# A block-recurrent attention and ELU-MLP kernel on one core: each engine's order from a table instead of a list scheduler

## Chip, cores and metric

The kernel runs on one core of one Trainium2 chip. The metric is the device time of one execution in microseconds (us), lower is better. The profile is one execution recorded by the hardware profiler. PE is TensorE's matmuls, PEld its weight loads, DVE is VectorE, ACT ScalarE, POOL GpSimd, SP SyncE; SP and, for three transfers, ACT issue the DMAs.

## What is computed

Eight batches of eight heads; 512 rows of x and 32 rows of state per head, 64 wide. Attention goes both ways, and the result feeds an MLP with an ELU between its two products.

```python
B, H, S, Ns, D = (8, 8, 512, 32, 64)
scores = scale * np.matmul(x, state.transpose(0, 1, 3, 2))      # softmax over the last axis -> a
xread = np.matmul(a, state)
scores2 = scale * np.matmul(state, x.transpose(0, 1, 3, 2))     # softmax over the last axis -> a2
sread = np.matmul(a2, x)
...
x = concatenate([xread, sread], axis=2), as (B * 544, 512)
h = x @ w_in                                                    # 512 -> 2048
g = np.where(h > 0.0, h, alpha * (np.exp(np.minimum(h, 0.0)) - 1.0))
return (g @ w_out).astype(np.float32)                           # 2048 -> 512
```

The two weights arrive as float64 and are turned into float32 words on the chip.

## The kernel before

The kernel folds the state rows into w_in: for a batch it first makes m = state x w_in (`make_m`, `make_three`, in four chunks of 512 columns of w_in), so that `ffn1` is softmax weights times m. `ffn1` and the second product `ffn2` use Strassen-like schemes: sums of blocks on DVE and POOL replace an eighth of the matmuls, and the second product does so twice (`Second`, steps named "second"). The parts are:

- `start()` (L1189): batches 0 and 1 plainly, while sixteen blocks of the weights arrive by DMA (1 MB each) and are converted by ACT and DVE (`convert`, L1129); converted w_in is written back to DRAM in eight halves for later fetches.
- `ffn2_1` (L1455), then `batch(b)` for b = 2 to 7 (L1522): `ffn1_chunk` four times, then `ffn2` (L1358), which also prepares batch b+1 at the boundary: scores, both softmaxes, x loaded anew, the transposed weights moved within SBUF by 16 small DMAs (`move_state`, L829), the state's read-out (`state_read`, L842), and its first chunks of m from fetched halves of w_in (`fetch`, L671).
- `states()` (L1634): the 256 state rows of all batches through the MLP.

None of these functions emits an instruction. Each records *steps* in `Plan` (L87), numbered in the order of recording: 2862 of them, 753 for PE, 1019 for DVE, 626 for ACT, 126 for POOL, 338 for SP. A step has an engine, an assumed cost, the steps that it depends on (from overlapping regions of its buffers), the PSUM banks that it opens or closes, and for a DMA its bytes and rate (`DMA_COST`, L23). A PE step is a group of matmuls, and each matmul call is two records in the profile (a "second" step is four calls, eight records).

`Plan.order` (L368) then makes up to three passes. `set_due` (L218) gives every step a due time, backwards from PE's steps laid end to end in the order of recording and from the steps that followed one another in a bank in the pass before. `run` (L241) plays the plan forward as a list scheduler: at each moment the engine that can start first takes a step that is ready, PE the one recorded earliest, POOL strictly in the order of recording, the others the one due earliest. PSUM banks are given out as the play goes on, the one that came free first to the next step that opens one. The pass that ends first in its own reckoning is kept, and its steps are emitted sorted by their planned start (L1712). The emission order is the order of every engine's queue; an engine runs its queue strictly in order. Where the play sees PE idle in its first 40 us, it puts filler matmuls (`fill`, L1703).

```python
for _, n, op in able[e]:
    if e == POOL and op is not in_turn[0]:
        continue
    ...
    if start <= at + 1e-9:
        return at, op
```

Steps that the prediction names, by number:

- Start. PE: 25 and 79 scores of batches 0 and 1; 58 state turned (batch 1); 73, 76 x turned (batch 1); 185, 187, 199, 201 turned softmax rows; 189, 203 read-outs; 65, 69, 118, 122 and 96, 100, 126, 130 the first eight tiles of ffn1 of batches 0 and 1; 111, 114, 141, 144, 155, 158, 229, 232 make_m, one half of w_in each. DVE: 26 to 41 softmax of batch 0 (37 its reciprocal, 38 and 40 multiply, 39 and 41 transpose); 107 part of a conversion; 59 copy of a turned state. ACT: 60 the other copy; 36 a sum ahead of the reciprocal; 66, 70, 71 ELU; 84, 88 exponentials of batch 1's softmax; 134 a conversion; 195, 196 exponentials of batch 1's row softmax, which 199 and 201 read.
- Batch 4. PE: 1374 make_three, 1383 state_read, 1445 the next make_three; SP: 1310 to 1325 move_state, 1402 to 1404 fetch; POOL: 1330 to 1333, 1379 to 1382, 1450 to 1457 sums of m.
- Batch 7's boundary. PE: 2353 to 2378 "second" steps; DVE: 2356 to 2375.

Of the kernel before, what the change touches and what calls it, by code (L numbers as in the profile page):

```python
# [20 lines left out]
PE, DVE, ACT, POOL, SP = "PE", "DVE", "ACT", "POOL", "SP"  # L21
# [13 lines left out]
def elements(ap):  # L35
    n = 1
    for k in ap.shape[1:]:
        n *= k
    return n


class Bank:
# [44 lines left out]
class Plan:  # L87
# [13 lines left out]
    def __init__(self, psum):  # L101
        self.psum, self.ops, self.banks, self.fixed = psum, [], [], []
        self.rows, self.writers, self.readers, self.masks = {}, {}, {}, {}
        self.places = {}

    def track(self, ap):
        self.rows[ap.tensor.name] = ap.ap[0][0]
# [88 lines left out]
    def prepare(self):  # L196
        for op in self.ops:
            op.users = []
            op.turn = self.places.get(op.number, op.number)
        for op in self.ops:  # L200
            for d in op.deps:
                d.users.append(op)
        self.opening = {}
        self.closing = {}
        for b in self.banks:
            self.opening.setdefault(b.first, []).append(b)
            self.closing.setdefault(b.last, []).append(b)
        self.kept = {}
        for b in self.fixed:
            self.kept.setdefault(b.first, []).append(b.fixed)  # L210
        self.all_banks = min([op.number for op in self.kept], default=0)
# [3 lines left out]
            return 0.1  # L215
        return self.LAG[a.engine].get(b.engine, 0.0)

    def set_due(self, after):  # L218
        at = 0.0
        for op in self.ops:  # L220
            op.due = 1e6 + op.number
        for op in sorted((op for op in self.ops if op.engine == PE), key=lambda op: op.turn):
            op.due = at
            at += op.cost
        follow = {}
        for a, b in after:
            follow.setdefault(a, []).append(b)
        for op in reversed(self.ops):
            took = op.cost
            if op.moved:  # L230
                took = op.cost + self.LANDING + op.moved / op.rate
            for u in op.users:
                op.due = min(op.due, u.due - self.lag(op, u) - took)
            for u in follow.get(op, ()):
                op.due = min(op.due, u.due - self.lag(op, u) - took)
            op.due -= op.nudge
        for op in self.ops:
            if op.rank is not None:
                op.due = op.rank - 1e6

    def run(self, until=0.0):  # L241

        waiting = {op: len(op.deps) for op in self.ops}
        ready = dict.fromkeys(self.ops, 0.0)
        free_at = dict.fromkeys(ENGINES, 0.0)
        for e in (PE, ACT, SP):
            free_at[e] = 0.7
        able = {e: [] for e in ENGINES}
        coming = {e: [] for e in ENGINES}
        banks = [(0.0, i) for i in range(self.BANKS)]  # L250
        fixed = {b.fixed for b in self.fixed}
        openers = sorted((op for op in self.ops if op in self.opening), key=lambda op: op.turn)
        oldest, opened = 0, set()
        in_turn = [op for op in self.ops if op.engine == POOL]
        holder, after, done, fills, lanes = {}, [], [], [], []
        port, holds, wire, shape, spare = 0.0, None, 0.0, None, None

        def release(op):
            heapq.heappush(coming[op.engine], (ready[op], op.number, op))

        def bank_time(op):

            if op in self.kept:
                free = [t for t, i in banks if i in self.kept[op]]
                return max(free) if len(free) == len(self.kept[op]) else None
            need = len(self.opening[op])
            if op is not openers[oldest] and op.number > self.all_banks:
                need += self.KEPT_BANKS
            free = choice(op)
            return free[need - 1][0] if need <= len(free) else None  # L270

        def choice(op):
            if op.number < self.all_banks:
                return banks
            return [b for b in banks if b[1] not in fixed]

        def pick(e):

            at = free_at[e]
            if not able[e] and coming[e]:  # L280
                at = max(at, coming[e][0][0])
            while able[e] or coming[e]:
                while coming[e] and coming[e][0][0] <= at + 1e-9:
                    _, n, op = heapq.heappop(coming[e])
                    bisect.insort(able[e], ((op.turn if e == PE else op.due), n, op))
                later = [coming[e][0][0]] if coming[e] else []
                for _, n, op in able[e]:
                    if e == POOL and op is not in_turn[0]:
                        continue
                    start = max(at, ready[op])  # L290
                    if op.port:
                        start = max(start, port + 0.01 * (e == POOL == holds))
                    if op in self.opening or op in self.kept:
                        t = bank_time(op)
                        if t is None:
                            continue
                        start = max(start, t)
                    if op.moved and len(lanes) >= 8:
                        start = max(start, lanes[-8] + 0.1)
                    if start <= at + 1e-9:  # L300
                        return at, op
                    later.append(start)
                if not later:
                    return None
                at = min(later)
            return None

        for op in self.ops:
            if not waiting[op]:
                release(op)  # L310
        while len(done) < len(self.ops):
            best = None
            for e in ENGINES:
                found = pick(e)
                if found and (best is None or found[0] < best[0] - 1e-9):
                    best = found + (e,)
            assert best is not None, "no operation is ready"
            at, op, e = best
            if e == POOL:
                in_turn.pop(0)  # L320
            able[e].remove(((op.turn if e == PE else op.due), op.number, op))
            if e == PE:
                t = free_at[PE]
                while at < until and t + 0.5 < at:
# [4 lines left out]
                        fills.append((t, spare.index, 1))  # L329
                    t += 0.3  # L330
            for bank in self.opening.get(op, ()):
                t, i = got = choice(op)[0]
                banks.remove(got)
                bank.index = i
                if i in holder:
                    after.append((holder[i], op))
                opened.add(op)
            if op in self.kept:
                banks = [b for b in banks if b[1] not in self.kept[op]]
                after += [(holder[i], op) for i in self.kept[op] if i in holder]  # L340
            while oldest < len(openers) and openers[oldest] in opened:
                oldest += 1
            if e == PE and (op.spare or op.name == "make_m"):
                spare = op.spare
            if e == PE and op.shape != shape:
# [11 lines left out]
            for u in op.users:  # L357
                ready[u] = max(ready[u], op.end + self.lag(op, u))
                waiting[u] -= 1
                if not waiting[u]:  # L360
                    release(u)
            for b in self.closing.get(op, ()):
                bisect.insort(banks, (op.end + self.LAG[op.engine].get(PE, 0.0), b.index))
                holder[b.index] = op
        self.after, self.fills = after, fills
        return done

    def order(self, passes, until=0.0):  # L368
        self.prepare()
        after = []  # L370
        best = None
        for _ in range(passes):
            self.set_due(after)
            try:
                done = self.run(until)
            except AssertionError:
                assert best is not None
                break
            last = max(op.end for op in done)
            after = self.after  # L380
            if best is None or last < best[0]:
                steps = [(op.start, op.number, op, op.end) for op in done]
                best = (last, sorted(steps), list(self.fills), [b.index for b in self.banks])
        self.last, steps, fills, index = best
        for b, i in zip(self.banks, index):
            b.index = i
        for at, n, op, end in steps:
            op.start, op.end = at, end
        return [s[2] for s in steps], fills

@with_exitstack
def kernel(
# [728 lines left out]
    def store(b, h, o):  # L1121
        rows = out_b[b, 0:S].rearrange("(p r) c -> p r c", r=R)
        dma(rows[:, 2 * h : 2 * h + 2], o.o_sb[h], kind="store")
        plan.ops[-1].nudge = 0

    def words(raw):
        return [raw.rearrange("p n (j w) -> p n j w", w=2)[:, :, :, i] for i in range(2)]

# [580 lines left out]
            )  # L1709
        )  # L1710

    steps, fills = plan.order(3, 40.0)  # L1712
    for op in steps:
        while fills and fills[0][0] <= op.start:
            fill(*fills.pop(0)[1:])
# [32 lines left out]
```

## Time and profile before

| what | value |
|---|---|
| median of 3 runs | 697.64 us (696.82 to 1012.53) |
| span of the profiled execution | 695.1 us, 14567 instructions |
| granted TensorE clock | 1.000 |
| PE, PEld, DVE, ACT, POOL busy | 684.7, 590.5, 572.4, 302.2, 112.7 us |
| first and last matmul | 1.36 us, last one ends at 690.4 us |
| DMA | 78.55 MB, 113 GB/s on the mean |

The profiled execution's own time is its span of 695.1 us and what lies around it, 2.5 us if it took as long as the median. In a line of the timeline, the columns are: start, length of the merged piece, engine, line, operation, what is written and read, how many records; in brackets the engine's idle time before it and what ended it. Nearly all instructions have line L466, since one helper emits them, so they are told apart by the buffers' names: ps is PSUM, sec, s, g, xr, aT, m, o, t_w, w_out, w_half and xe are parts of the on-chip buffer. L1706 is the filler. In a table by stage each engine has its busy time and, in brackets, its number of records; the last three columns are the granted clock, the DMA share and GB/s. A group's line ends with its busy time, the mean length of one in ns, and the idle time ahead of it.

### The profile page before, as it was taken

The page shows a single profiled execution, that of the slowest core. Times are in us where ns is not written, and L with a number is a line of the kernel's source. Part 1 is how long each engine was busy: PE and PEld are TensorE (multiplying, and loading weights), DVE is VectorE, ACT ScalarE, POOL GpSimd, SP SyncE. Part 2 cuts the span into 40 slices and gives each one's busy share as a digit, 9 for nine tenths or more (in the row PEclk, how much of TensorE's full clock was granted, in tenths as well). Part 3 has the DMA queues.
Part 4 walks back from the last instruction along what each step waited for, and adds up shares of the span by engine and source line. Part 5 has one row for each costly group of instructions (what it writes and reads, how often), then busy time and mean ns, then how long its engine had stood idle before and what let it go on. Part 6 is the DMA issues. An engine that isn't in the chain of part 4 may idle for free.

```text
span 695.1 us, 14567 instructions
## 1 busy us (share of the span) xinstructions
PE 684.7 (98%) x5782; PEld 590.5 (85%) x5782; DVE 572.4 (82%) x1019; ACT 302.2 (43%) x640; POOL 112.7 (16%) x133
## 2 busy tenths in 40 slices
PE   8999999999999999999999999999999999999997
PEld 7544468889988998889988998899888998899996
DVE  4999899979949994999679995999499966997640
ACT  4999883003057213732275215731373217600530
POOL 0200000002430151104230143015110423000000
PEclk9999999999999999999999999999999999999999
DMA  8858774202281507440572218250745043200300
GB/s 222 271 190 260 255 219 99 61 31 91 72 223 41 122 19 235 83 122 4 167 166 74 50 39 244 53 123 18 240 77 123 1 154 122 61 1 32 122 8 24
DMA packets 111268, 78.55 MB, mean 113 GB/s; under 512 B 89184, under 2 KB 92768, under 8 KB 111200
## 3 DMA queue, kind: packets, MB, share of 16 engines
q1 hardware_dynamic: 108988, 77.06, 39.6%
q8 instruction: 46, 0.75, 0.5%
q10 hardware_dynamic: 2212, 0.56, 0.4%
q14 instruction: 22, 0.18, 0.1%
HBM read 61.34 MB, written 13.11 MB: 107 GB/s over the span
## 4 chain that ended last, share of the span: by engine, by line
PE 90%; ACT 4%; DMA 4%; DVE 1%; issue 1%; ACTq 0%
PE ps L466 90%; ACT sec L466 2%; DMA xe<-in_x_dram 1%; DMA t_w<-in_moe_w_out_dram 1%; DMA g<-in_x_dram 1%; ACT t_w L466 1%; DVE w_half L466 0%; ACT o L466 0%; DVE t_w L466 0%; DVE sec L466 0%; ACT w_half L466 0%; ACTq L466 0%; ACT g L466 0%; ACT m L466 0%; ACT s L466 0%
## 5 line engine op out<-in xcount | busy, mean ns | idle before, releaser
L466 PE MATMUL ps<-aT,m 128*128 128x256 f32 (+1 forms) x568 | 147.9, 405 | 0.2
L466 PE MATMUL ps<-w_out,g 128*128 128x128 f32 (+1 forms) x864 | 144.2, 314 | 0.0
L466 PEld LDWEIGHTS ps<-w_out,g 128*128 128x128 f32 x864 | 126.3, 191 | 12.4 <-issue 4.2
L466 PEld LDWEIGHTS ps<-aT,m 128*128 128x128 f32 x568 | 106.2, 190 | 29.6 <-issue 14.1
L466 DVE TENSOR_TENSOR o<-o,ps 128x128 f32<-128x128 f32 (+2 forms) x239 | 67.3, 286 | 41.2 <-PE ps L466 40.5
L466 ACT COPY o<-ps 128x128 f32<-128x128 f32 (+2 forms) x70 | 23.1, 335 | 145.6 <-PE ps L466 139.6
L466 POOL TENSOR_TENSOR xr<-xr,small 128x512 f32<-128x512 f32 x24 | 30.0, 1271 | 335.1 <-DVE small L466 171.3
L466 PE MATMUL ps<-sec 128*128 128x128 f32 x560 | 74.8, 277 | 0.0
L466 PEld LDWEIGHTS ps<-sec 128*128 128x128 f32 x560 | 68.5, 192 | 4.0 <-DVE o L466 3.7
L466 POOL TENSOR_TENSOR m<-m 128x256 f32<-128x256 f32 x72 | 60.5, 861 | 27.1 <-ACT m L466 25.7
L466 PE MATMUL ps<-t_w,s 128*128 128x128 f32 (+1 forms) x432 | 64.5, 298 | 0.0
L466 ACT ACTIVATE xe<-ps 128x512 f32<-128x512 f32 x96 | 54.9, 602 | 19.4 <-PE ps L466 12.8
L466 PEld LDWEIGHTS ps<-t_w,s 128*128 128x128 f32 x432 | 58.6, 192 | 2.5
L466 ACT COPY m<-ps 128x512 f32<-128x512 f32 (+1 forms) x56 | 28.1, 540 | 61.0 <-PE ps L466 60.9
L466 DVE SCALAR_TENSOR_TENSOR g<-xe,ps 128x512 f32<-128x512 f32 x66 | 43.9, 682 | 9.8 <-DMA w_half<-w_in_mem 5.8
L466 DVE TENSOR_TENSOR ps<-sec,ps 128x512 f32<-128x512 f32 (+1 forms) x52 | 34.9, 671 | 14.1 <-ACT sec L466 7.2
L466 ACT COPY sec<-ps 128x512 f32<-128x512 f32 (+1 forms) x52 | 29.7, 571 | 28.6 <-PE ps L466 28.5
L466 PE MATMUL ps<-aT,s 128*128 128x256 f32 x168 | 41.2, 379 | 0.0
L466 ACT ACTIVATE xe<-xe 128x512 f32<-128x512 f32 x66 | 39.8, 636 | 0.7
L466 PEld LDWEIGHTS ps<-aT,s 128*128 128x128 f32 x168 | 31.9, 190 | 4.3
L466 PE MATMUL ps<-w_half,kT 64*32 64x256 f32 x1024 | 34.9, 381 | 0.7 <-DVE xe L466 0.4
L466 PE MATMUL ps<-sec,g 128*128 128x128 f32 (+1 forms) x252 | 31.5, 272 | 1.2 <-DMA g<-in_x_dram 1.2
(149 smaller groups left out, 1111.6 us busy)
## 6 DMA issues: line engine op xcount, KB each, us to landing
w_half<-w_in_mem SPq DMA_DIRECT2D x54, 512.0 KB
t_w<-in_moe_w_out_dram SPq DMA_DIRECT2D x8, 1024.0 KB
t_w<-in_moe_w_in_dram SPq DMA_DIRECT2D x7, 1024.0 KB
out_dram<-o SPq DMA_DIRECT2D x14, 512.0 KB
xe<-in_x_dram SPq DMA_DIRECT2D x26, 256.0 KB
o<-in_x_dram SPq DMA_DIRECT2D x80, 64.0 KB
w_in_mem<-w_half SPq DMA_DIRECT2D x8, 512.0 KB
xr<-xr SPq DMA_DIRECT2D x96, 32.0 KB
```

Of the source, the lines that this page charges most:

```text
L466: ins = getattr(engine, name)(**named)
```

## The change

`Plan.order` with `set_due` and `run` goes. A table `ORDERS` holds, for each of the five engines, all its steps' numbers in the order in which they are to stand. `Plan.follow` plays the plan forward once: each engine takes the next step of its list when that is ready, banks are given out as before, and the steps are emitted sorted by planned start. The steps themselves, their buffers, their number and the transfers stay. POOL no longer follows the order of recording.

```diff
+ORDERS = {
+    PE: in_order(
+        "16 19 22 55 25 73 58 76 185 187 61 79 65 111 114 189 69 122 118 199 201 96 126 100 130 141 144 203 158 "
+        "155 166 162 174 232 229 210 170 206 214 218 246 243 289 254 270 250 258 301 292 304 308 262 320 274 278 "
...
+        "1228 1230 1232 1250 1265 1236 1248 1267 1234 1269 1338 1254 1271 1340 1273 1252 1275 1343 1277 1347 1345 1357 "
+        "1349 1351 1359 1374 1362 1364 1366 1368 1370 1423 1386 1388 1391 1421 1393 1395 1397 1399 1383 1424 1425 "
+        "1445 1430 1460 1458 1432 1437 1461 1462 1486 1467 1488 1489 1469 1474 1495 1490 1510 1497 1538 1513 1514 "
...
+    DVE: in_order(
+        "44 45 50 51 46 47 17 52 53 21 24 26-28 32 179 178 31 106 35 108 37 59 38 40 39 41 107 184 109 80-82 86 "
...
+    ACT: in_order(
+        "1 5 7 42 43 49 18 48 20 23 57 104 105 30 56 34 180 60 74 181 36 75 182 183 78 77 188 135 63 64 186 66 "
+        "134 117 67 112 116 190 113 84 88 194 70 90 191 71 195 196 119 148 120 222 202 97 98 149 197 200 127 123 "
...
+    POOL: in_order(
...
+        "957 959 996 995 1043 1114 1116 1044 1045 997 1115 1118 1119 1117 1120 1046 1121 1330 1284 1288 1293 1295 "
+        "1331 1332 1379 1450 1333 1451 1380 1452 1454 1455 1381 1382 1453 1456 1457 1620 1624 1666 1668 1629 1631 "
...
+    SP: in_order(
+        "2 3 0 4 6 10 11 8 12 9 13-15 54 115 62 110 140 145 154 159 228 233 247 242 288 300 353 346 375 356 389 "
...
+        "1212 1305 1304 1217 1218 1307 1306 1310 1325 1312 1314 1402 1319 1403 1322 1404 1323 1316 1313 1321 1320 "
+        "1324 1311 1317 1318 1315 1373 1401 1407 1411 1547 1420 1406 1414 1412 1416 1408 1417 1405 1409 1410 1418 "
...
-    def set_due(self, after):
...
-    def run(self, until=0.0):
...
+    def follow(self, orders, until=0.0):
+
+        self.prepare()
...
+        line = {e: [self.ops[n] for n in orders[e]] for e in ENGINES}
+        at_op = dict.fromkeys(ENGINES, 0)
...
+        def soonest(e):
+
+            if at_op[e] == len(line[e]) or waiting[line[e][at_op[e]]]:
+                return None
+            op = line[e][at_op[e]]
+            at = max(free_at[e], ready[op])
...
+            return at, op
...
-    steps, fills = plan.order(3, 40.0)
+    steps, fills = plan.follow(ORDERS, 40.0)
     for op in steps:
```

In the order before, PE's start runs 16 19 22 55 58 25 61 73 76 187 185 79 189 65 111 114 69 118 122 199 201 96, and the 16 moves 1310 to 1325 stand together on SP, ahead of the fetches 1402 to 1404.

## Prediction

> **What bounds the kernel now.** First the page's busy times and its chain of waits:
>
> ```profile
> PE 684.7 (98%) x5782; PEld 590.5 (85%) x5782; DVE 572.4 (82%) x1019; ACT 302.2 (43%) x640; POOL 112.7 (16%) x133
> ...
> PE 90%; ACT 4%; DMA 4%; DVE 1%; issue 1%; ACTq 0%
> ```
>
> TensorE (PE) carries 90% of the chain. Whether its busy time is full work is read from the timeline of PE, at a place in the middle, from where one group starts to where the next one does:
>
> ```profile
> 382.95 1.06 PE L466 MATMUL ps<-t_w,g 128*128 128x128 f32 x8
> 383.84 1.06 PE L466 MATMUL ps<-sec,sec 128*128 128x128 f32 x8
> 384.73 1.06 PE L466 MATMUL ps<-sec,g 128*128 128x128 f32 x8
> ```
>
> Eight matmuls start every 0.89 us, so 0.112 us each, with no break, though each needs another weight. Then the busy times of each engine by stage (start to 11.25 us, to 36.41, to 80, to 158, to the last matmul, the end):
>
> ```profile
> 11.25:36.41 25.16, 22.10 (x290) 13.49 (x291) 23.27 (x38) 21.49 (x47) 4.11 (x4) 1.00 0.87 256
> 36.41:80.00 43.59, 43.09 (x339) 19.20 (x337) 40.46 (x54) 40.06 (x77) 0.00 (x0) 1.00 0.69 219
> ...
> 158.00:690.40 532.40, 532.04 (x4750) 486.22 (x4748) 432.70 (x832) 208.39 (x468) 107.87 (x122) 1.00 0.35 95
> ```
>
> The second number is PE. From 36.41 us on it idles 0.50 + 0.36 us in 654 us. The holes lie ahead of that. PE's timeline there (L1706 are the filler matmuls):
>
> ```profile
> 15.41 2.50 PE L1706 MATMUL ps<-sec 128*128 128x128 f32 x20
> ...
> 19.32 0.65 PE L466 MATMUL ps<-sec,g 64*128 64x64 f32 x14 [1.21 <-DMA g<-in_x_dram]
> 19.89 1.16 PE L1706 MATMUL ps<-sec 128*128 128x128 f32 x8
> ...
> 24.63 1.10 PE L466 MATMUL ps<-xe,xr 128*32 128x64 f32 x64
> 25.66 1.98 PE L466 MATMUL ps<-aT,m 128*128 128x512 f32 x4
> ...
> 34.45 0.39 PE L1706 MATMUL ps<-sec 128*128 128x128 f32 x2
> 35.70 0.66 PE L466 MATMUL ps<-sec,s 128*128 128x128 f32 x4 [0.86 <-ACT s L466]
> 36.19 0.39 PE L1706 MATMUL ps<-sec 128*128 128x128 f32 x2
> ```
>
> From the landing of x (11.25) to 36.41 PE idles 25.16 - 22.10 = 3.06 us and fills 2.50 + 1.16 + 0.39 + 0.39 = 4.44 us: 7.5 us. With the two lone holes below, 1.2 us, everything that an order can win back behind the landing of x is 8.7 us, 1.25% of the time.
>
> The Trainium skill speaks for more: "Perfetto Trace Analysis", section "Identifying the Most-Contended Engine", judges PE's headroom by its weight-load time and not by matmul time. By that figure, 85% here, 15% of the span or 104 us would be open. The even starts above contradict it: PE's own rate is the limit in this stage, and the measurement decides.
>
> **The change part by part.** All operations, buffers and transfers stay; 575 of 753 PE steps, 896 of 1019 on DVE, 487 of 626 on ACT, 96 of 126 on POOL and 289 of 338 on SP stand at another place. Both programs issue 47 filler calls (94 records). I add up PE's line, since it ends the span. The profiled execution is 695.1 us long, 2.5 us below the median of 697.64; I add the sum to both.
>
> *Start, up to the first matmul of batch 1's second half (step 96, at 36.41).* The same steps precede it in both orders. The first softmax sets when step 65 starts (25.66): in its chain on DVE the table takes out one conversion step (107, 0.63 us long) and puts in the copy 59 (0.23); ACT gets copy 60 (0.21) ahead of the sum that the reciprocal waits for. Net -0.2. The read-out 189, 1.03 us (24.63 to 25.66), which filled a wait, now follows steps 111 and 114, behind the softmax: +1.03. It eats into the wait of 201 (34.61 to 35.70, 1.1 us), which sits behind ACT's exponentials 195 and 196: ACT's own queue now has 134, 66, 70, 71, 84, 88 ahead of them, of 0.6 to 1.2 us each, so I let 0.9 of the 1.1 go. Sum -0.1; bounds -1.3 (read-out still covered, whole wait gone) and +0.8 (no wait gone). SP moves the first weight halves ahead of a 32 KB state load and the next weight block ahead of x of batch 1; the bytes ahead of x of batch 0 hardly change: 0.
>
> *36 to 158.* Steps 232 and 229 move up by some four tiles. PE reaches them at 36.41 plus 7 tiles of 1.72 and 3.6 of short steps, 52.0; the conversion that they need ended at 49.90 and stands one place earlier on DVE: 2 us of cover, 0. If it were gone, a wait on DVE's 1.2 us steps would cost up to that much.
>
> *Two lone holes.* PE's timelines around 62 and 498:
>
> ```profile
> 62.94 1.52 PE L466 MATMUL ps<-w_half,kT 64*32 64x256 f32 x46 [0.33 <-DVE g L466]
> ...
> 499.09 0.67 PE L466 MATMUL ps<-w_half,kT 64*32 64x256 f32 x16 [0.35 <-DVE xe L466]
> ```
>
> Each waits for a bank that DVE frees, and start to start each costs 0.6 us. In the table other steps stand in front. Bounds -1.2 and 0; I take half, -0.6. A change between tiled and full matmuls costs 0.1 us (the eight matmuls behind make_three take 331.62 to 332.62, 1.00 instead of 0.89); counted in the two orders, such changes go from 79 to 80: +0.1.
>
> *SP in a batch.* Its timeline at one boundary:
>
> ```profile
> 253.56 10.80 SPq L466 DMA_DIRECT2D xr<-xr  x16
> 264.46 1.48 SPq L466 DMA_DIRECT2D w_half<-w_in_mem  x3
> ```
>
> Now two or three of these fetches stand among the 16 moves, and a fetch waits until make_three has read its buffer, with up to 12 moves queued behind it. From make_three's end to the read-out 1383 PE has 12 steps of 0.893 and two of 0.864: 12.4 us. Behind the fetch: 12 x 0.675 + 3 x 0.49 = 9.6, and at most 3.5 us of landing (last move issued at 263.8, its reader began at 267.3): 13.1. Cost 0 to 0.7 a batch, five batches, 0 to 3.5. I take 0: the 3.5 is an upper limit, for nothing in PE's waits names that landing.
>
> *DVE at the boundaries.* The table leaves less slack. The tightest place is ahead of step 2378 of batch 7: from the end of 2353 PE has ten steps of 0.893 and make_three of 1.46, 10.4 us. In it DVE, once ACT's copy is done, has 7 small adds (0.20 start to start), 4 transposes (0.63), 8 sums (0.60) and one of 0.34: 9.05, and the hand-overs take some 0.8. That leaves 0.5. The rows of this same boundary show that a sum can take longer:
>
> ```profile
> 557.66 0.68 DVE L466 TENSOR_TENSOR s<-s,sec 128x512 f32<-128x512 f32 x1
> ...
> 561.82 1.21 DVE L466 TENSOR_TENSOR g<-g 128x512 f32<-128x512 f32 x1
> ```
>
> Two such (+0.53 each) make it 0.5 late. Over six boundaries: 0 to about 6 x 0.9 = 5.4; I take 0.2 each, +1.2, since other boundaries are looser.
>
> "SBUF — State Buffer" of the Trainium skill, section "SBUF: two separate sides", speaks against the change here: DVE with two SBUF inputs and POOL lock each other out for a whole instruction. If all of POOL's 112.7 us blocked DVE, DVE would be busy 685 us of 695. The rows show 0.53 for single ones.
>
> *POOL.* In batch 4 the sums of make_three 1445 stand ahead of sum 1381. From 1445's end to its reader PE has 8 steps of 0.864, 6.9 us; POOL has 8 sums of 0.735 (the s row) to 0.861 (the m row), 5.9 to 6.9, and 1 us of copies and hand-overs before. Cost 0 to 1.0; I take 0.2.
>
> Sum: -0.1 - 0.6 + 0.1 + 0 + 1.2 + 0.2 = +0.8. Span 695.9, time 697.64 + 0.8 = 698.4. All low ends: -2.4, 695.2; all high ends: +0.8 + 0.1 + 3.5 + 5.4 + 1.0 = +10.8, 708.4.
>
> **The rivals.** (1) *The table closes the holes of the start.* For: 7.5 us are there. Against: they hang on one softmax chain, of which only 0.4 us leaves. Half of it and both lone holes: -3.8 - 1.2, 692.6; all: 688.9. (2) *Thin slack on DVE and POOL.* Waits at every boundary, near the high ends: +5 to +11, 702.6 to 708.4; against it, the margins of most places stay positive. (3) *Slower by more than 2%: moves behind fetches.* Three fetches of 512 KB at 244 GB/s (a busy slice of the page) take 6.4 us; if the last move's data waited that long, the read-out would come 9.6 + 6.4 + 3.5 - 12.4 = 7.1 us late, in five batches 35.5 us, 733.1. It decides as soon as fetch data is still queued when the last move is issued and the delay passes 2.8 us a batch. Against: the last move is issued some 7 us behind the last early fetch. (4) *The table changes nothing that runs*: ruled out, the five instruction lists differ.
>
> **How the numbers follow.** Forecast 0.68, its own range 695.2 to 702.0. Rival 1 0.13, rival 2 0.14, rival 3 0.04, anything else 0.01. The range leaves out rival 3, the upper part of 2 and the lower part of 1: 692.5 to 705.0. Over 2% (14.0 us, about what a measurement of this kernel can tell from no change) faster would need more than the 8.7 us above, so x landing earlier too: 0.01. Slower by over 2% is rival 3 and a sliver of 2: 0.04. Within 2%: 0.95.
>
> **What would show it.** PE idle of 3 us and 4.4 of fills again before step 96, at 36.3; no 0.33 idle at 62 and 498; PE waits for DVE o or POOL m of under 1 us at boundaries; the read-out matmuls (xe,xr) without a wait for a DMA. A start that reaches step 96 before 34 would make it wrong, or a wait for xr that repeats in each batch.

## Result, and the profile after

| | before | table |
|---|---|---|
| median | 697.33 us (6 runs) | 700.35 us (6 runs, 698.37 to 700.88) |
| ratio | | 1.0043, 95% interval 1.0031 to 1.0054 |
| span of the profiled execution | 695.1 | 697.4 (own time 699.22) |
| last matmul ends | 690.42 | 689.41 |
| behind the last matmul | 4.7 | 8.0 |

The table makes the kernel 3 us slower by the ratio, though PE is done 1.0 us sooner. One of before's six runs took 1012.53 us, and the ratio leaves it out. The page after, busy times and chain:

```profile
PE 684.5 (98%) x5782; PEld 590.1 (85%) x5782; DVE 565.6 (81%) x1019; ACT 303.4 (44%) x640; POOL 109.3 (16%) x133
...
PE 84%; DVE 5%; DMA 3%; SPq 3%; ACT 2%; issue 1%; POOL 0%; DVEq 0%
```

No engine works longer but ACT, by 1.2 us. PE's share of the chain fell from 90% to 84%, and SP's queue is in it with 3%, where before had none. By stage, in the table's own bounds (start, span, then PE's busy time first; last three columns clock, DMA share, GB/s):

```profile
10.88:34.39 23.51, 21.65 (x288) 12.83 (x289) 21.70 (x38) 19.59 (x46) 4.11 (x4) 1.00 0.83 262
34.39:80.00 45.61, 44.88 (x343) 19.75 (x342) 42.05 (x54) 44.17 (x81) 0.00 (x0) 1.00 0.66 209
...
158.00:689.40 531.40, 530.64 (x4704) 486.03 (x4696) 425.13 (x831) 208.93 (x469) 104.46 (x122) 1.00 0.36 96
689.40:697.50 8.10, 0.01 (x1) 0.00 (x0) 0.00 (x0) 0.37 (x1) 0.00 (x0) 0.78 0.21 66
```

The last row of before, which the prediction left out:

```profile
690.40:695.20 4.80, 0.02 (x1) 0.00 (x0) 0.00 (x0) 0.37 (x1) 0.00 (x0) 0.95 0.09 27
```

Step 96 starts 23.51 us after x lands (25.16 before). In the long stage PE idles 0.76 us (0.36 before). In the last row PE has nothing to do, and DMA moves 66 GB/s for 8.1 us instead of 27 for 4.8.

**The start.** PE's timeline from the wait for x of batch 1 to step 96 (L1770 is the filler):

```profile
14.77 2.40 PE L1770 MATMUL ps<-sec 128*128 128x128 f32 x20
...
18.58 1.43 PE L1770 MATMUL ps<-sec 128*128 128x128 f32 x8 [0.71 <-ACT m L531]
...
23.16 1.09 PE L531 MATMUL ps<-o,kT 64*32 64x512 f32 x16
24.19 1.98 PE L531 MATMUL ps<-aT,m 128*128 128x512 f32 x4
26.10 1.09 PE L531 MATMUL ps<-w_half,kT 64*32 64x256 f32 x32
27.13 1.10 PE L531 MATMUL ps<-xe,xr 128*32 128x64 f32 x64
28.19 5.42 PE L531 MATMUL ps<-aT,m 128*128 128x512 f32 x12
33.45 1.11 PE L531 MATMUL ps<-sec,s 128*128 128x128 f32 x8
34.39 2.41 PE L531 MATMUL ps<-s,g 128*128 128x512 f32 x5
```

The first softmax's user, step 65, starts at 24.19 (25.66 before), the read-out (xe,xr) stands behind it, and from 28.19 on there is neither a wait nor a filler; before had a wait of 0.86 us and two fillers there. DVE's chain ahead of step 65, first before, then after:

```profile
22.00 0.34 DVE L466 RECIPROCAL sec<-sec 128x32 f32<-128x32 f32 x1
22.27 0.63 DVE L466 TENSOR_SCALAR w_half<-w_half 128x1024 uint32<-128x1024 uint32 x1
22.81 1.28 DVE L466 TENSOR_TENSOR sec<-sec 128x512 f32<-128x512 f32 x2
24.01 1.29 DVE L466 STREAM_TRANSPOSE aT<-sec 128x512 f32<-128x512 f32 x2
```

```profile
21.23 0.35 DVE L531 RECIPROCAL sec<-sec 128x32 f32<-128x32 f32 x1
21.49 0.16 DVE L531 COPY kT<-ps 128x64 f32<-128x64 f32 x1
21.61 1.29 DVE L531 TENSOR_TENSOR sec<-sec 128x512 f32<-128x512 f32 x2
22.82 1.30 DVE L531 STREAM_TRANSPOSE aT<-sec 128x512 f32<-128x512 f32 x2
```

Counted from where x lands (11.25 and 10.88), the reciprocal is 0.40 us sooner, from it to the product it is 0.38 instead of 0.81, and step 65 follows the second transpose by 0.07 instead of 0.36, because the read-out is out of the way: 0.40 + 0.43 + 0.29 = 1.12 us.

**The middle.** The lead of PE's line, comparing the same place in both lines, is 2.02 us at step 96, 2.74 at PE's place 181 (its 182nd step, at 200 us, ahead of which both lines have done the same steps) and 1.00 at the end. What is given back stands at the boundaries. The read-outs of batches 4 and 5 after:

```profile
342.14 0.30 PE L531 MATMUL ps<-xe,xr 128*32 128x64 f32 x2
342.71 1.21 PE L531 MATMUL ps<-xe,xr 128*32 128x64 f32 x62 [0.27 <-DMA xr<-xr]
...
418.07 0.30 PE L531 MATMUL ps<-xe,xr 128*32 128x64 f32 x2
418.54 1.28 PE L531 MATMUL ps<-xe,xr 128*32 128x64 f32 x62 [0.17 <-DMA xr<-xr]
```

Two matmuls run and the other 62 wait for a move (xr<-xr). Start to start the read-out takes 1.72 and 1.69 us instead of 1.03.

How much cover there was is read from the trace's semaphores, counters that a DMA raises when it lands. In before the last move lands 1.8 to 1.9 us behind its issue (3.4 in the first of these batches) and 0.8 to 2.1 us ahead of the read-out: at 340.42 for 342.48, at 416.12 for 417.69. In the table the last moves of batches 4, 5 and 6 land at 342.58, 418.50 and 493.96, that is 0.44, 0.43 and 0.06 us behind the read-out's start. There are two ways to that. In batch 4 the move is issued 2.15 us later than in before (340.75) and lands in 1.8 us. In batches 5 and 6 it stands on SP just behind a fetch of 512 KB and lands 3.3 and 3.1 us after its issue; those fetches land at 418.14 and 493.56, 0.4 us ahead of it. Batch 6's read-out takes 1.21 us, and make_three near 572 waits 0.2 us for w_half.

**The end.** SP's timeline over the last 10 us, before and after:

```profile
687.45 3.94 SPq L466 DMA_DIRECT2D out_dram<-o  x2
```

```profile
688.18 2.51 SPq L531 DMA_DIRECT2D out_dram<-o  x4
```

Before has two of the last four quarter results (128 KB each) already under way. The table has one first (2851) that waits for the sum 2850, which ends at 688.15; the other three are queued behind it, and all four are issued within 2.5 us. Their packets run one store after the other from 689.45 on, and end at 691.4, 692.8, 694.2 and 695.7, 1.4 us apart.

### The profile page after: what moved, and what is told of

Same layout as the page of the kernel before. It is cut to its first block, busy times and chain, and to the rows that moved or that the text cites. A ratio compares the mean times of both kernels' runs of the same rounds, so it can differ in the third digit from the quotient of the medians.

```text
span 697.4 us, 14417 instructions
## 1 busy us (share of the span) xinstructions
PE 684.5 (98%) x5782; PEld 590.1 (85%) x5782; DVE 565.6 (81%) x1019; ACT 303.4 (44%) x640; POOL 109.3 (16%) x133
## 4 chain that ended last, share of the span: by engine, by line
PE 84%; DVE 5%; DMA 3%; SPq 3%; ACT 2%; issue 1%; POOL 0%; DVEq 0%
PE ps L531 84%; SPq L531 3%; DVE sec L531 2%; DMA w_half<-w_in_mem 1%; DMA xe<-in_x_dram 1%; ACT sec L531 1%; DVE o L531 1%; DMA xr<-xr 1%; DVE g L531 1%; DVE aT L531 1%; DVE s L531 0%; DVE small L531 0%; DVE xr L531 0%; ACT t_w L531 0%; ACT w_half L531 0%
## 5 line engine op out<-in xcount | busy, mean ns | idle before, releaser
L531 PE MATMUL ps<-w_out,g 128*128 128x128 f32 (+1 forms) x864 | 150.1, 315 | 0.0
L531 PE MATMUL ps<-aT,m 128*128 128x256 f32 (+1 forms) x568 | 150.1, 406 | 0.0
L531 PEld LDWEIGHTS ps<-aT,m 128*128 128x128 f32 x568 | 105.4, 190 | 29.3 <-issue 13.5
L531 DVE TENSOR_TENSOR o<-o,ps 128x128 f32<-128x128 f32 (+2 forms) x239 | 64.7, 285 | 44.1 <-PE ps L531 37.6
L531 POOL TENSOR_TENSOR xr<-xr,small 128x512 f32<-128x512 f32 x24 | 33.3, 1402 | 267.0 <-DVE small L531 178.2
L531 POOL TENSOR_TENSOR m<-m 128x256 f32<-128x256 f32 x72 | 54.3, 770 | 130.3 <-ACT m L531 129.5
L531 PE MATMUL ps<-t_w,s 128*128 128x128 f32 (+1 forms) x432 | 69.2, 299 | 0.0
L531 ACT ACTIVATE sec<-ps 128x512 f32<-128x512 f32 (+1 forms) x40 | 22.4, 566 | 22.1 <-PE ps L531 10.2
```

Of the source, the lines that this page charges most:

```text
L531: ins = getattr(engine, name)(**named)
```

## Experiments

In the texts on record, theory A is named anew for each run. A lead or loss is against before's trace at the same place of PE's line.

**e1_tail**: the table with before's order of the last four stores.

```diff
-SP: ... 2851 2809 2841 2861
+SP: ... 2809 2841 2851 2861
```

> The table with one change: on SP the last four stores stand in the order in which their data are ready (2809, 2841, 2851, 2861), so that 2851 is no longer ahead of 2809 and 2841. Theory A (the table gains 1.0 us by PE's last matmul and loses 3.3 us behind it, because two stores that were ready long before wait behind 2851 and four transfers of about 1.5 us then follow one another): 3.3 us less than the table, 697.0, span about 694.1, last matmul still at 689.4. Rival B (the time behind the last matmul is not a matter of SP's order; the loss lies in the waits at the batch boundaries): no change, 700.0 to 700.7.

Measured: 696.48 us, ratio 1.0001 (0.9991 to 1.0011), so 0.42% or 2.9 us below the table; span 694.7, last matmul at 689.63, 5.0 us behind it. SP and the last stage:

```profile
688.39 2.21 SPq L536 DMA_DIRECT2D out_dram<-o  x2
```

```profile
689.63:694.70 5.07, 0.00 (x0) 0.00 (x0) 0.00 (x0) 0.37 (x1) 0.00 (x0) 0.74 0.17 52
```

Four numbers at the end of SP's list make the whole difference between slower and the same.

**e2_before_tail_late**: before's order, with the table's last four stores.

```diff
-SP: ... 2809 2841 2851 2861
+SP: ... 2851 2809 2841 2861
```

> The order of the kernel before, all five engines, with SP's last four stores as the table has them (2851, 2809, 2841, 2861). The same displacement alone, where 2850 ends 3.0 us ahead of PE's end instead of 1.3. Theory A with the transfers one after another at 1.45 us: three start at 688.5, the last one lands at 694.3 instead of 693.9: +0.4 us, 697.7. Theory A', that the displacement costs 3.3 us wherever it stands: 700.6. Rival B: 697.3.

Measured: 698.33, ratio 1.0022 (1.0011 to 1.0032), +1.5 us; 5.9 us behind the last matmul. Neither size was right. The span ends 8.9 us after the four stores are released by 2850 (687.28 to 696.18); in the table it is 9.3 us (688.15 to 697.43). So the stores set the end in both, and what they cost is how late 2850 ends: in the table it ends 1.3 us ahead of PE's last matmul, in before's order 3.0.

**e3_start_table**: the table up to PE's place 181 (200 us) on all lines, before's order from there.

```diff
-ORDERS[e] = table
+ORDERS[e] = table up to place 181, then before's order of the rest
```

> The table's order up to about 200 us (the first 181 PE steps and what the other engines do up to there), then the order of the kernel before, its tail included. Theory A: the lead of 2.7 us that the table has at that point (200.1 against 197.3) is kept to the end: 694.6. Rival C: the lead is lost because DVE or the transfers bind the later stages: 696.5 to 697.3.

Measured: 696.94, ratio 1.0009 (0.9995 to 1.0022). The expected gain did not come. A wait of 0.72 us sits at the seam (197.8, for ACT's kT); the lead is 1.55 us at place 181 and 0.27 at the end, because now make_three comes too early for its fetched weights:

```profile
420.98 0.66 PE L536 MATMUL ps<-w_half,kT 64*32 64x256 f32 x16
422.24 1.10 PE L536 MATMUL ps<-w_half,kT 64*32 64x256 f32 x32 [0.59 <-DMA w_half<-w_in_mem]
```

In all it waits 1.3 us for w_half there and near 497; before's trace has no such wait, but before's order is not free of them: in e2_before_tail_late make_three waits 0.8 us for w_half near 195. So the lead drops by 1.0 us at the seam and by 1.3 behind it, and the time is within rival C's range.

**e5_moves**: e1_tail, with the 16 moves of each boundary together again, ahead of the fetches.

```diff
-SP: ... 1655 1654 1659 1649 1651 1738 1650 1652 1646 1740 1648 1647 1656 1657 1661 1658 1739 1660 1653
+SP: ... 1655 1654 1659 1649 1651 1650 1652 1646 1648 1647 1656 1657 1661 1658 1660 1653 1738 1740 1739
```

> The table with SP's tail mended as in e1_tail, and at every batch boundary the 16 moves together again, ahead of the fetches that the table put among them. Theory D (the read-out's wait for the moves, 0.5 us in batch 4 and 0.4 in batch 5, comes from the fetches standing in front of the last moves): 0.9 less than e1_tail, about 696.1, and no wait inside the read-out's matmuls. Rival: the moves are late because DVE's transposes ahead of them are, then as e1_tail, 697.0; or the fetches now come late for make_three, then above 697.

Measured: 702.36, ratio 1.0082 (1.0069 to 1.0095). The waits for xr are gone, and make_three waits for w_half six times, 4.7 us, most at its first boundary:

```profile
194.86 1.06 PE L536 MATMUL ps<-w_out,g 128*128 128x128 f32 x8
198.44 1.53 PE L536 MATMUL ps<-w_half,kT 64*32 64x256 f32 x48 [2.53 <-DMA w_half<-w_in_mem]
```

So placing fetches among the moves is needed for the rest of the table's order. The profiled execution (703.95) also lost 3.3 us at 55 to 62 us, where the edit changes nothing; see the last section.

**e6_softmax_chain**: e1_tail with conversion 107 back in the softmax chain.

```diff
-DVE: ... 35 108 37 59 38 40 39 41 107 184 109
+DVE: ... 35 108 37 59 107 38 40 39 41 184 109
```

> e1_tail with conversion 107 (0.54 us start to start on DVE) put back between the reciprocal 37 and the product 38 of the first softmax, as before has it. Theory A, the softmax chain sets step 65 and all behind it: step 65 starts 0.5 us later than in e1_tail (13.15 us after x lands there, 14.41 in before), step 96 also 0.5 later. Rival B, something else ends last there (the copies on ACT, the scores): step 65 later by under 0.15. The end moves by 0 to 0.5 in both.

Measured (one execution, 697.71): from the landing of x, step 65 comes at 13.49 us (13.15 in e1_tail) and step 96 at 23.60 (23.35): +0.34 and +0.25. Step 65 lies between both expectations. The six executions with the table's start as it is (after, e1, e3, e5, e8, e10) have step 65 at 13.15 to 13.35 and step 96 at 23.35 to 23.57, so only the effect on step 65 stands outside their spread, by 0.14: 107 in the chain costs, but not its full 0.54, and what is left of it at step 96 is not shown.

**e7_readout_first**: e1_tail with the read-out 189 ahead of step 65, and its copy 186 ahead of conversion 135.

```diff
-PE: ... 61 79 65 111 114 189 69
+PE: ... 61 79 189 65 111 114 69
-ACT: ... 188 135 63 64 186 66
+ACT: ... 188 186 135 63 64 66
```

> e1_tail with the read-out 189 (and the copy 186 that it needs) put back ahead of step 65. The prediction's premise, the read-out fills a wait ahead of 65 for nothing and costs 1.03 us behind it: step 65 as in e1_tail (24.46 us, 13.15 after x lands), step 96 up to 1.0 earlier. Theory A, the operands of 65 are done when it starts, so the read-out holds it up: step 65 1.0 us later, the 1.07 us behind step 114 gone, step 96 within 0.3 of e1_tail.

Measured (one execution, 699.19), PE's timeline:

```profile
25.21 1.10 PE L536 MATMUL ps<-xe,xr 128*32 128x64 f32 x64
26.25 1.98 PE L536 MATMUL ps<-aT,m 128*128 128x512 f32 x4
28.16 1.09 PE L536 MATMUL ps<-w_half,kT 64*32 64x256 f32 x32
30.21 5.42 PE L536 MATMUL ps<-aT,m 128*128 128x512 f32 x12 [0.96 <-ACT g L536]
```

Step 65 comes 1.06 us later from x (14.21 against 13.15), so here the read-out holds it up. The second half failed: step 96 is 1.02 later too, because where the read-out stood PE now waits 0.96 us for ACT's copies (g). The table's place for the read-out fills a real wait behind step 114; the place of before delays step 65.

**e8_act_fetch** and **e9_before_act_fetch**: the fifteen fetches among the moves of five boundaries issued from ACT's queue, behind a copy; e8 on e1_tail, e9 on before's order.

```diff
+    if len(plan.ops) in BY_ACT:
+        queue = ACT
-SP: ... 1310 1325 1312 1314 1402 1319 1403 1322 1404 1323
+SP: ... 1310 1325 1312 1314 1319 1322 1323
-ACT: ... 1376 1378
+ACT: ... 1376 1402 1403 1404 1378
```

> The table with its last four stores in the order of before (e1_tail: 696.48 us, last matmul ends 689.63), and the three 512 KB fetches of w_in halves that stand among the 16 moves at the boundaries of five batches (at about 254, 330, 406, 480 and 557 us) issued from ACT's queue, behind a copy, instead of SP's. Theory A, SP's line of 16 moves and 3 fetches gives back what the start won: no wait for xr at the read-outs of 342, 418 and 492 us (0.2 to 0.6 us each in e1_tail), none for w_half; last matmul at about 688.5, time about 695.3, 1.1 to 1.2 below e1_tail. Rival B, the given-back time hangs on DVE and on the order, and the transfers only came last: waits go to DVE or ACT at the same places, last matmul 689.4 to 689.7, time 696.3 to 696.6. Rival C, the fetches run sooner beside the moves and take their bandwidth: waits for xr grow, above 697.

> The order of before in every line, with the same fifteen fetches issued from ACT's queue. Theory A, the fetches matter only to a line that comes earlier than the order of before: its trace has no wait for xr or w_half over 0.3 us there, so 0 to -0.3 us, 696.4 to 696.8. Rival B, SP's line holds the order of before back as well: 695.6 or less. Rival C, the sooner fetches slow the moves: above 697.

Measured: 701.43, ratio 1.0063 (1.0047 to 1.0080), and 700.07, ratio 1.0045 (1.0034 to 1.0057). Both are slower. ACT's timeline at e8's first boundary, then SP's in e1_tail:

```profile
252.66 0.59 ACT L537 COPY m<-ps 128x512 f32<-128x512 f32 x1 [1.71 <-PE ps L537]
252.72 7.83 ACTq L537 DMA_DIRECT2D w_half<-w_in_mem  x3
260.65 0.65 ACT L537 COPY s<-ps 128x256 f32<-128x256 f32 x2 [7.41 <-DMA xr<-xr]
```

```profile
254.02 0.53 SPq L536 DMA_DIRECT2D w_half<-w_in_mem  x1
```

The piece of 7.83 us is no work of that length: the view merges three issues with the time between them. One by one they are:

```profile
252.72 0.35 ACTq L537 DMA_DIRECT2D w_half<-w_in_mem  x1
254.29 0.36 ACTq L537 DMA_DIRECT2D w_half<-w_in_mem  x1
260.22 0.33 ACTq L537 DMA_DIRECT2D w_half<-w_in_mem  x1
```

Each takes 0.33 to 0.36 us, less than SP's 0.53, and between them ACT's queue waits 1.2 and 5.6 us. The pieces of 5.3 and 4.8 us at the next two boundaries are made up in the same way. The semaphores in the trace say what for. The program's transfers take eight semaphores in turn, whichever queue issues them. The second fetch has the semaphore of a move that SP issued at 252.37 and that lands at 254.23. The third has that of a move issued at 254.90, which lands only at 260.12, behind two of the fetches (256.76 and 259.72): 5.2 us after its issue instead of 1.9. ACT's next copy, queued behind the fetches, starts at 260.65, so the releaser named for it, xr<-xr, is the cause, and PE waits for that copy:

```profile
261.08 2.07 PE L537 MATMUL ps<-aT,m 128*128 128x256 f32 x4 [3.41 <-ACT s L537]
```

PE loses 5.0 us at this boundary, 3.41 of it in this row and most of the rest in waits of 1.0 and 0.55 us behind it. In e9 the second fetch of each of the five boundaries waits 4.1 to 5.2 us in the same way. Rival C has the sign and the first half of its way, since moves do land later behind fetches. The second half is mostly another: e8's read-outs take 1.03 us throughout, three of e9's take 1.21, 1.41 and 1.18 (0.7 us in all), and the time goes in ACT's queue. No run gives the fetches semaphores of their own, so this account is read from the trace alone.

The Trainium skill, "Perfetto Trace Analysis", section "DMA Optimizations", says that balancing DMAs over several issuing engines may help where descriptor generation is the limit. No run here shows that SP's issues are a limit; with the fetches on ACT the kernel takes 4.3 us longer (e8 against e1_tail, 0.62%) and 3.1 (e9 against before). The same page, section "DMA Instruction — HWDGE (DVE, Sync)", says that the generator is locked for exclusive use and that the profiled length of an issue holds the wait for the lock. At this boundary the three lengths of 0.33 to 0.36 us show no such wait.

**e4_rest_table**: before's order up to place 181, the table with the mended tail from there.

```diff
-ORDERS[e] = table
+ORDERS[e] = before's order up to place 181, then the table's order of the rest
```

> The order of before up to PE's place 181 (200 us) on all lines, from there the table's, with the last four stores in the order of before. Theory A, the table's part behind 200 us costs some 1.6 us by itself, whatever the start gave (from place 181 to the last matmul the four table runs give back 1.55, 1.74, 1.68 and 1.49 us at leads of -2.3, -2.7, -1.2 and +0.3): last matmul at 690.4 + 1.6 = 692.0 for an x that lands at 11.25, tail 5.0, span 697.0, time 698.4. Rival B, the later part has limits of its own that eat a lead and cost nothing without one: last matmul at 690.4 or sooner, time 696.5 to 697.

Measured: 699.86, ratio 1.0040 (1.0026 to 1.0054); place 181 at +0.58, last matmul at 692.97, +2.55. The time is 1.5 us above theory A's 698.4. Without any lead to eat the table's later part gives back 2.0 us:

```profile
420.74 0.30 PE L536 MATMUL ps<-xe,xr 128*32 128x64 f32 x2
421.36 1.28 PE L536 MATMUL ps<-xe,xr 128*32 128x64 f32 x62 [0.32 <-DMA xr<-xr]
```

Not the same read-outs wait as in the table: batch 4's takes 1.03 us here, batch 5's 1.84, and batch 6's starts 0.7 us late and takes 1.40. So the table's order pays behind 200 us with no lead at all (theory A). That a lead meets a limit too is not ruled out, since e3 loses 1.3 of its 1.55 us on before's order. The leads of single executions:

| run | lead at step 96 | at place 181 | at the last matmul | given back from 181 | behind the last matmul |
|---|---|---|---|---|---|
| table | 2.02 | 2.74 | 1.00 | 1.7 | 8.0 |
| e1_tail | 1.75 | 2.34 | 0.79 | 1.6 | 5.0 |
| e6_softmax_chain | 0.92 | 1.20 | -0.48 | 1.7 | 5.0 |
| e7_readout_first | 0.00 | -0.34 | -1.82 | 1.5 | 5.2 |
| e4_rest_table | -0.15 | -0.58 | -2.55 | 2.0 | 5.1 |
| e3_start_table | 1.93 | 1.55 | 0.27 | 1.3 | 4.7 |

About 1 us of such a lead is the execution and not the order. In these rows x lands at 10.88, 11.31, 11.89, 12.04, 11.68 and 11.12 us, in before at 11.25, and before's own order led before's trace by 0.49 at step 96 and was 0.44 behind at place 181 in e2, and led by 0.83 there in e9. The medians against before agree with the table of leads in this: table's start with before's rest (e3) +0.6 us, an interval that holds no change, before's start with the table's rest (e4) +2.8, both of the table (e1) +0.1. So what the start is worth hangs on what stands behind it.

**e10_one_fetch**: e1_tail with one (batch 4) or two (5 and 6) of the three fetches put behind the last move.

```diff
-SP: ... 1651 1738 1650 1652 1646 1740 1648 1647 1656 1657 1661 1658 1739 1660 1653
+SP: ... 1651 1738 1650 1652 1646 1648 1647 1656 1657 1661 1658 1660 1653 1740 1739
```

> The table with the last four stores in the order of before (e1_tail), and of the three w_in fetches among the moves in batches 4, 5 and 6 one (batch 4) or two (5, 6) put behind the last move, so that the last move is issued 0.6 or 1.2 us sooner. Theory A, the read-out waits for the last move in SP's line, and make_three has 1 to 2 us of cover for one or two late fetches (it has none for three, which cost 0.35 to 0.6): the waits at 418 and 492 us shrink by 0.4 to 0.6 each, that at 342 by 0.2, no wait for w_half above 0.2; last matmul about 1.0 sooner than in e1_tail (689.63 for an x that lands at 11.31), time 695.4. Rival B, make_three waits as much instead: 696.3 to 696.7. Rival C, the read-out's wait is not the last move's: waits stay, 696.5.

Measured: 696.31, ratio 0.9991 (0.9980 to 1.0002). PE at batch 5's boundary:

```profile
419.03 1.10 PE L536 MATMUL ps<-xe,xr 128*32 128x64 f32 x64
...
422.35 1.53 PE L536 MATMUL ps<-w_half,kT 64*32 64x256 f32 x48 [0.30 <-DMA w_half<-w_in_mem]
```

The read-out no longer waits, and make_three waits instead, 0.30 us here; near 497 us its next step comes 0.9 us late, with no releaser shown. From place 181 on 1.25 us is given back instead of 1.55. Theory A has the mechanism, rival B most of the size. It is the best version here, and its interval still holds "no change".

## Why the prediction was right or wrong

The forecast was 698.4 us, the time is 700.35: inside its range and on its likeliest case, within 2%. The sum behind it was right only as a total, by luck: a gain of 2 us at the start that it did not see and a loss of 3.3 behind the last matmul that it did not price nearly cancel. In the profiled executions (span 695.14 to 697.43, +2.3):

| term | predicted | measured |
|---|---|---|
| start, to step 96 | -0.1 | -2.0, of it -0.4 by x landing sooner in this execution |
| 36 to 200 us | -0.3 (hole at 62) | -0.7 |
| hole at 498 | -0.3 | -0.6, not shown to be the order's |
| moves and fetches on SP | 0 (0 to 3.5) | +1.6 (waits at 342, 418, 492 and 572) |
| DVE and POOL at boundaries | +1.4 | +0.2 at 329, no wait for POOL m |
| gradual, not tied to one wait | +0.1 (shape changes) | +0.5 |
| behind the last matmul | not in the sum | +3.3 |

- **The step that failed: "I add up PE's line, since it ends the span."** PE's line does not end the span: 4.7 us of stores follow it in before, and the change also reorders SP's last four. The prediction counted 289 moved steps on SP and priced only the first weight loads and the boundaries. e1_tail shows that the tail alone is 2.9 us, as much as the whole slowdown.
- **Start, mis-sized.** The chain was to lose 0.2 us and lost 0.8, and step 65 another 0.3, for three reasons. Between reciprocal and product the prediction set lengths against each other (0.63 out, 0.23 in) and added ACT's 0.21, while start to start it is 0.54 against 0.12. ACT's sum 36 got sooner, by a copy that no longer stands ahead of it. And the read-out that "filled a wait" ahead of 65 held 65 up by 0.3. The wait of 201 went as predicted, all of it instead of 0.9, and the fillers beside it too; the read-out behind step 114 takes 1.06 us, but costs only about 0.1, for e7_readout_first waits 0.96 for ACT's copies where it stands. Net of x the start gained 1.65 us against before's profile, more than the bound of 1.3; before's profile is the slowest of the four executions of that start (step 96 at 24.62 to 25.16 us behind x), so the gain is 1.1 to 1.8. Step 96 came at 34.39, 0.4 above the time set as proof of error. Rival 1 had this right in part: 1.8 of the 7.5 us of idling and fillers from the landing of x went (5.7 are left, 1.86 + 3.83).
- **Moves and fetches, the mechanism right and taken at 0.** The text's own working gave 0 to 0.7 a batch, with the last move down at most 13.1 us behind make_three's end. In batches 4, 5 and 6 of the table it is down 13.2, 13.0 and 13.5 us behind it (8.7 in before), and by PE's lead these three cost 0.6, 0.55 and 0.3. It took 0 because before's waits named no such landing, and because 3.5 us of landing was only an upper limit. The landing itself, 1.8 to 1.9 us in before, and the cover of 0.8 to 2.1 us were there to be measured. The sign "without a wait for a DMA" failed in two batches. Rival 3's mechanism is seen in batches 5 and 6, where the last move lands behind a fetch issued just ahead of it, but it costs 1.3 us of landing, not 6.4, and part of that is covered.
- **DVE, over-sized.** PE waits 0.2 us once for DVE o. The tight places of the prediction held. The lock-out that the cited port rule names does show. With POOL idle (542.75 to 549.24 us) a 128x512 sum within SBUF takes 0.69 us; the one of 1.21 us at 561.82 that the prediction shows starts beside POOL, which runs until 562.48:

```profile
544.50 0.69 DVE L466 TENSOR_TENSOR g<-g 128x512 f32<-128x512 f32 x1
```

```profile
558.72 3.76 POOL L466 TENSOR_TENSOR m<-m 128x256 f32<-128x256 f32 x4 [3.12 <-ACT m L466]
```

In before's whole trace 205 such sums with POOL idle take at most 0.71 us, and 37 beside POOL 0.91 on the mean; with an operand in PSUM they take at most 0.70 either way. In all, 41 DVE instructions are over 0.1 us longer than others of their kind, 16.0 us together, each beside an instruction of POOL. In the table only 12 are, 4.9 us together, and DVE is busy 6.8 us less. The prediction took the lock-out as it was in before and did not ask whether the new order changes it. That this is what kept the tight places in time is likely, but no run varies it alone.
- **Two lone holes**, one of them shown. The hole at 62 is gone with the table and still there in e2, e4 and e9, which have before's start; it is worth the 0.6 us that the prediction put on it, of which it took half. The hole at 498 is gone too, but before's own order has none there in e2 and e9.

## What to carry to other kernels

Add up to the end of the span, not to the last matmul: for every queue that a reorder touches, look at its last few entries and ask what the first of them waits for, since everything behind it waits too. Where a wait's cover is not named in the trace, measure it as the time from the landing to its first reader, and set the new order's landing against it. A merged piece of a timeline can hold waits, so read its records one by one before calling an operation slow. A gain at the start counts only beside what the rest of the order costs, and the seam experiment (one order up to a place where both have done the same steps, the other behind it) tells these apart.

## What the runs showed of the hardware

- A small DMA behind large ones lands late. The last move of 32 KB lands 1.8 to 1.9 us after its issue in all but one batch of before, 3.1 to 3.3 behind a 512 KB fetch in the table, and 5.2 behind two of them in e8_act_fetch.
- A transfer can wait in its queue for an earlier one of another queue that has the same semaphore: 5.6 us on ACT in e8_act_fetch, where the issue itself takes 0.33.
- DVE's sums of two operands in SBUF are held up by POOL: 0.69 us with POOL idle, 0.91 on the mean beside it in before.
- Four 128 KB stores issued within 2.5 us (table) and 3.9 us (e2_before_tail_late) let the span end 9.3 and 8.9 us behind their release.
- The same order does not take the same time. Over twelve profiled executions x lands between 10.67 and 12.04 us. And the table has a thin place that shows it: ACT's conversion near 53 us waits until the write-back of a half of w_in has left its buffer. Before has no wait there; the eight runs with the table's order there have it, 0.4 to 2.5 us. e1_tail and e5_moves, whose lines are the same up to there:

```profile
53.04 1.17 ACT L536 ACTIVATE w_half<-t_w 128x1024 f32<-128x1024 f32 x1 [0.54 <-DMA w_in_mem<-w_half]
```

```profile
54.73 1.14 ACT L536 ACTIVATE w_half<-t_w 128x1024 f32<-128x1024 f32 x1 [2.50 <-DMA w_in_mem<-w_half]
```

The store that is waited for is issued at 44.58 and 44.30 us and lands at 52.95 and 54.65, each 1.2 to 1.3 us behind a 1 MB load of a weight block that was issued 0.4 us ahead of it (44.16 to 51.72, and 43.89 to 53.38). So it comes late with that load. Up to 0.8 us of the wait PE waits for 0.4 us at most, beyond that 1.0 to 2.0 (e7_readout_first, e10_one_fetch, e5_moves). Why the load takes 7.6 us in one and 9.5 in the other stays open, and so do differences of about 1 us between two single profiles.
